# Chunked attention and a squared-ReLU feed-forward on one core: store queues, score slots, and the share of early Strassen differences

## The chip, the cores and the metric

The kernel runs on one core of one Trainium2 chip. Its engines have queues of their own and run side by side: PE (TensorE, matmuls and transposes), DVE (VectorE), ACT (ScalarE), POOL (GpSimd) and SP (SyncE, which here only issues DMAs). The metric is the device time of one execution in microseconds, and the number that counts is the median of the runs.

## The reference

Attention within chunks of 64 tokens comes first; its heads are laid side by side and go through a feed-forward layer with a squared ReLU. There are 8 sequences of 576 tokens, 8 heads of 64, a model width of 512, and 2048 hidden features.

```python
scores = scale * np.matmul(q_c, k_c.transpose(0, 1, 2, 4, 3))   # chunks of 64 x 64
attn = softmax(scores)
x = np.matmul(attn, v_c)            # -> (4608 tokens, 512)
h = np.maximum(x @ w_in, 0.0)       # w_in: 512 x 2048
out = h * h @ w_out                 # w_out: 2048 x 512, float32
```

## The kernel before

**Tiling.** The 4608 tokens form 18 groups of 256 tokens (4 chunks each), and two groups form a block: nine blocks of 512 tokens, 0 to 8. While PE computes the feed-forward layer of block j, the attention of block j+1 is woven in, and the q, k and v of block j+2 are loaded.

**One block.** `ffn_in` (line 392) has 16 units, one for each tile of 128 hidden features: four matmuls of 512 columns accumulate over the model width (line 399), ACT takes the ReLU out of PSUM (line 410), and the square is written to `gT` in bf16, by DVE (line 415) or for three of the tiles by ACT (line 413). The ReLU results have three buffers, the PSUM banks of the units four. From block 2 on, the tiles are taken in the order `FT_EARLY`, in which a few tiles of the lower and the upper half of the hidden features come first.

`ffn_out` (line 436) multiplies by `w_out` with one level of a Strassen scheme: seven products of quarter size, each of 16 matmuls in two steps of eight (line 466). Five of them take a difference of two quarters of `gT` as their left side: d5, d2, d1, d6, d7, in the order in which they are wanted. DVE makes these differences (`difference`, line 384) into tiles called `w_st`. A part of each, the first `N_EARLY` of its eight feature tiles, is made within `ffn_in`, in the queue behind the square of unit 8 (lines 417 to 420). The rest is made at the start of `ffn_out` and between its products (`rest_of`, line 445). The products are, in order, a22 into bank n, a11 into bank m, d5 into n, d2 into m, d1 into n, d6 into m, d7 into n. Between them the banks are read out: n1 and n2 by ACT, the sum w and the output quarters c21, c12 and c22 by DVE (line 431), c11 by ACT (line 546). Each quarter of the output is stored as soon as it is made (`store`, line 482).

**Block 0 and block 1** differ: block 0 uses plain matmuls for the output (`ffn_out_by_ft`), block 1 runs `ffn_in` in two halves of 256 columns and 32 shorter units.

**Attention steps of a group.** In the code: C casts q and k to bf16 (on POOL for groups under 8, else on ACT); TD transposes them with a DMA on SP (line 268; the first groups are transposed by PE instead: TA, TE, TQ, TK); SC computes the scores and ACT takes their exponentials (lines 291 and 302); AV multiplies by the values and DVE divides by the row sums, two steps for each half group, which I call a value division (lines 318, 325, 326); XT transposes the result to `xT`, the input of the next block's `ffn_in` (by PE and a copy for groups under 6, lines 345 and 350; by a DMA on SP from there on, line 339).

**The order of the work** is written out by hand. Each yield of `ffn_in` and `ffn_out` is a slot, and a table gives the slot behind which each attention step is put. Slots 0 to 15 follow the units of `ffn_in`, and 16 to 29 the half products of `ffn_out`. From block 2 on the table is this (the two numbers are those of the two groups); one load is issued on SP at each slot named in `go_slots`:

```python
slots = {SC: (8, 8), AV: (11, 15), XT: (14, 18), C: (18, 20), TD: (20, 23)}
if j == 2:
    slots = {SC: (8, 10), AV: (12, 15), XT: (15, 18), C: (20, 23), TD: (22, 25)}
```

SP issues all loads and the DMA transposes in program order. The stores of the output are issued by POOL; in the last block, where each quarter is stored in two halves of 128 tokens or at once, the two halves of c11 go out on ACT and SP.

Of the kernel before, what the change touches and what calls it, by code (L numbers as in the profile page):

```python
# [17 lines left out]
def kernel(  # L18
# [9 lines left out]
    nc = tc.nc  # L28

    B, H, S, D = q.shape  # L30
# [4 lines left out]
    n_hp = H // 2  # L35
# [296 lines left out]
    def transpose_x(g):  # L332
        j, c = place[g]
        if j not in xTs:
            xTs[j] = att_pool.tile([128, BT // 128, n_dt, 128], BF16, name="xT", bufs=2)
        x = state.pop(("x", g))
        dst = xTs[j][:, c // 128:c // 128 + 2].rearrange("p t h q -> p (t h) q")
        if g >= FIRST_DMA_X:
            nc.sync.dma_start_transpose(out=dst, in_=x.rearrange("p t h a d -> p (t h a d)"))
            return  # L340
        ps = ps_att.tile([128, 1024], FP32, name="ps_att")
        psb = ps.bitcast(BF16)[:, 0:1024].rearrange("p (b q) -> p b q", q=128)
        for t in range(2):
            for hp in range(n_hp):
                nc.tensor.transpose(  # L345
                    out=psb[:, t * n_hp + hp, :],
                    in_=x[:, t, hp].rearrange("p a d -> p (a d)"),
                    identity=ident)
        copy = nc.vector.tensor_copy if g == blocks[1][0] else nc.scalar.copy
        copy(out=dst, in_=psb)  # L350

    C, TD = cast_qk, transpose_qk_dma
    SC, AV, XT = scores, values, transpose_x
# [31 lines left out]
    FT_ORDER = [*range(n_ft // 2, n_ft), *range(n_ft // 2)]  # L385


    N_EARLY = 2
    FT_EARLY = [ft + h for ft in range(N_EARLY) for h in (n_ft // 2, 0)]
    FT_EARLY += [ft for ft in FT_ORDER if ft not in FT_EARLY]  # L390

# [44 lines left out]
    def ffn_out(j):  # L436

        last = j == len(blocks) - 1
        a11, a12, a21, a22 = quarters(j)

        def rest_of(name):
            difference(j, name, slice(N_EARLY if (name, j) in state else 0, HF))
            return state[name, j]

        n_tt = HT // 128
        banks = {}  # L450

        def chain(name):
            tiles = [ps_ffn.tile([128, 512], FP32, name="ps_ffn")
                     for _ in range(n_tt if last else 1)]
            banks[name] = [(tiles[t], 0, HD, t) for t in range(n_tt)] if last else [
                (tiles[0], 0, n_tt * HD, None)]
            return [tiles[t][:, 0:HD] if last else tiles[0][:, t * HD:(t + 1) * HD]
                    for t in range(n_tt)]

        def product(name, a, b, first):  # L460
            if first:
                state["chain", name] = chain(name)
            outs = state["chain", name]
            for t in range(n_tt):
                for i in range(HF):
                    nc.tensor.matmul(  # L466
                        out=outs[t],
                        lhsT=a[:, i, t * 128:(t + 1) * 128],
                        rhs=b[:, i, :],
                        start=(first and i == 0 and (last or t == 0)), stop=(i == HF - 1),  # L470
                        skip_group_check=True)
                yield

        def parts(name):
            for tile_, lo, n, t in banks[name]:
                at_ = (t or 0) * HD
                yield tile_[:, lo:lo + n], slice(at_, at_ + n), t

        def kept(name):
            return ffn_pool.tile([128, n_tt * HD], FP32, name=name)  # L480

        def store(dma, o_sb, half, col, t):
            g = blocks[j][half]
            b, s0 = chunks[g][0]
            t0 = b * S + s0
            if not is_whole(g):

                for p in range(2):
                    dma.dma_start(
                        out=out.rearrange("(b s) d -> s b d", s=S)[  # L490
                            s0:s0 + CH, b + p:b + 4:2, col:col + HD],
                        in_=o_sb[p * CH:(p + 1) * CH].rearrange("p (t d) -> p t d", d=HD))
            elif t is None:
                dma.dma_start(  # L494
                    out=out[t0:t0 + HT, col:col + HD].rearrange("(t p) d -> p t d", p=128),
                    in_=o_sb.rearrange("p (t d) -> p t d", d=HD))
            else:
                dma.dma_start(
                    out=out[t0 + t * 128:t0 + (t + 1) * 128, col:col + HD],
                    in_=o_sb[:, t * HD:(t + 1) * HD])  # L500

        def o_tile():
            return ffn_pool.tile([128, n_tt * HD], FP32, name="o_sb", bufs=4)

        d5 = rest_of("d5")
        d2 = rest_of("d2")
        yield from product("n", a22, b11_p_b21, True)
        n1 = kept("n1")
        for ps, cols, t in parts("n"):
            nc.scalar.copy(out=n1[:, cols], in_=ps)  # L510
        yield from product("m", a11, b12_p_b22, True)
        w = kept("nm")
        for ps, cols, t in parts("m"):
            add(nc.vector, w[:, cols], ps, n1[:, cols])
        d1 = rest_of("d1")
        yield from product("n", d5, b22, False)
        n2 = kept("n2")
        for ps, cols, t in parts("n"):
            nc.scalar.copy(out=n2[:, cols], in_=ps)
        d6 = rest_of("d6")  # L520
        if j == 1:
            d7 = rest_of("d7")
        yield from product("m", d2, b11, False)
        c21 = o_tile()
        for ps, cols, t in parts("m"):
            add(nc.vector, c21[:, cols], w[:, cols], ps, ALU.subtract)
            store(nc.gpsimd, c21, 1, 0, t)
        if j > 1:
            d7 = rest_of("d7")
        yield from product("n", d1, b11_m_b22, False)  # L530
        s = kept("n1")
        for ps, cols, t in parts("n"):
            add(nc.vector, s[:, cols], ps, n2[:, cols], ALU.subtract)
        c12 = o_tile()
        add(nc.vector, c12, w, n2, ALU.subtract)
        store(nc.gpsimd, c12, 0, HD, None)
        yield from product("m", d6, b11_p_b12, False)
        c22 = o_tile()
        for ps, cols, t in parts("m"):
            add(nc.vector, c22[:, cols], ps, s[:, cols])  # L540
            store(nc.gpsimd, c22, 1, HD, t)
        yield from product("n", d7, b21_p_b22, False)
        c11 = o_tile()
        for ps, cols, t in parts("n"):
            copy = nc.vector.tensor_copy if t else nc.scalar.copy
            copy(out=c11[:, cols], in_=ps)  # L546
            store(nc.gpsimd if t is None else nc.sync if t else nc.scalar, c11, 0, 0, t)

    def ffn_out_by_ft(j):

# [76 lines left out]
    for j, grps in enumerate(blocks):  # L627
# [15 lines left out]
        elif j == 1:  # L643
            loads = itertools.chain(*map(v_pieces, nxt), *map(qk_pieces, far))
            go_slots = [*range(22, 27), *range(28, 48)]
            for slot, f in ((1, TK), (4, SC), (7, AV), (12, XT)):
                at(slot, f, grps[1])
            for i, g in enumerate(nxt):
                for slot, f in ((16 + 4 * i, C), (21 + 6 * i, TD), (36 + i, SC), (38 + 2 * i, AV),
                                (41 + 2 * i, XT)):  # L650
                    at(slot, f, g)
            for i, g in enumerate(far):
                at(36 + 4 * i, C, g)
                at(42 + 3 * i, TD, g)
            at(2, sum_quarters(b11_p_b12, b11, b12), None)
            at(12, sum_quarters(b12_p_b22, b12, b22), None)
            at(20, sum_quarters(b21_p_b22, b21, b22), None)
            phases = [ffn_in(1, [(0, 256, FT_ORDER), (256, 256, FT_ORDER)]), ffn_out(1)]
        else:
            loads, go_slots = pieces(far), range(32)  # L660
            slots = {SC: (8, 8), AV: (11, 15), XT: (14, 18), C: (18, 20), TD: (20, 23)}
            if j == 3:
                go_slots = [*range(6), *range(13, 32)]
            if j == 2:
                loads = itertools.chain(*map(v_pieces, nxt), loads)
                slots = {SC: (8, 10), AV: (12, 15), XT: (15, 18), C: (20, 23), TD: (22, 25)}
                go_slots = [*range(16), 23, 24, *range(26, 36)]
            for f in (SC, AV, XT):
                for i, g in enumerate(nxt):
                    at(slots[f][i], f, g)  # L670
            for f in (C, TD):
                for i, g in enumerate(far):
                    at(slots[f][i], f, g)
            phases = [ffn_in(j, [(0, BT, FT_EARLY)]), ffn_out(j)]
        slot = 0
# [41 lines left out]
```

## Time and profile before

| what | us |
|---|---|
| median of 9 runs (lowest, highest) | 284.67 (283.17, 290.31) |
| the profiled execution | 283.25 |
| its span, from the first to the last instruction | 281.1 |
| PE busy | 268.7 |
| DVE busy | 189.4 |
| ACT busy | 161.6 |
| POOL busy | 55.6 |

Times within the profile are in us from the start of the span. Block 2 starts on PE at 82.85, block 3 at 110.84, block 4 at 138.88, block 5 at 166.97, block 6 at 195.00, block 7 at 223.04 and block 8 at 251.07; from block 3 on they are 28.03 to 28.09 apart. A line of the groups gives source line, engine, operation, output and inputs, shapes and count, then the busy time and the mean of one in ns, then the idle time before. A line of waits gives the waiting engine and line, what it waited for, and the total, the number of times and the longest wait. Waits are told by the instruction that waited; a name with a q (SPq, POOLq) is the queue that issues.

### The profile page before, as it was taken

How to read it: one execution, taken by the hardware profiler on the slowest of the kernel's cores; microseconds unless marked ns; L12 is line 12 of the kernel's file. 1: busy time of each engine (PE TensorE's matmuls, PEld its weight loads, DVE VectorE, ACT ScalarE, POOL GpSimd, SP SyncE). 2: the span in 40 equal slices, each digit the busy share in tenths (PEclk: the TensorE clock that was granted, in tenths of full speed). 3: DMA queues.
4: the chain of work that ended last, by engine and by line, in shares of the span. 5: the costliest groups of instructions: out<-in, count | busy, mean ns of one | idle time of the engine just before them, and what ended most of it. 6: DMA issues, size and time to landing. Idle time of an engine off the chain costs nothing.

```text
span 281.1 us, 7197 instructions
## 1 busy us (share of the span) xinstructions
PE 268.7 (96%) x2951; PEld 175.3 (62%) x2954; DVE 189.4 (67%) x338; ACT 161.6 (58%) x277; POOL 55.6 (20%) x92
## 2 busy tenths in 40 slices
PE   1999999999999999999999999999999999999994
PEld 1554444778774487448744874487448744874583
DVE  1254614899953885599559955995599559955982
ACT  1558705786349763976197619761976197119610
POOL 2038834240170003000400040004000400060012
PEclk9999999999999999999999999999999999999999
DMA  7999999999999999989999899669897980341003
GB/s 202 241 327 332 373 352 246 312 227 214 228 224 251 224 219 190 247 188 227 218 281 235 189 244 263 118 140 225 212 248 174 212 163 10 67 113 39 0 38 113
DMA packets 140816, 57.09 MB, mean 203 GB/s; under 512 B 110640, under 2 KB 137520, under 8 KB 140784
## 3 DMA queue, kind: packets, MB, share of 16 engines
q1 hardware_dynamic: 137744, 47.33, 76.6%
q0 software_dynamic: 2896, 9.18, 10.1%
q8 instruction: 23, 0.38, 0.6%
q10 hardware_dynamic: 144, 0.13, 0.1%
q14 instruction: 9, 0.07, 0.1%
HBM read 36.70 MB, written 9.44 MB: 164 GB/s over the span
## 4 chain that ended last, share of the span: by engine, by line
PE 58%; DVE 23%; ACT 7%; issue 4%; SPq 4%; DMA 2%; POOL 0%; ACTq 0%; DVEq 0%
PE ps_ffn L466 27%; PE ps_ffn L399 24%; DVE gT L415 10%; ACT rl L410 6%; DVE x L326 6%; DVE w_st L384 6%; PE ps_ffn L556 5%; DMA w_st<-in_moe_w_in_dram 2%; SPq L106 1%; SPq L148 1%; SPq L152 1%; DVE rec L325 1%; ACT gT L413 1%; PE ps_att L345 1%; PE ps_att L291 1%
## 5 line engine op out<-in xcount | busy, mean ns | idle before, releaser
L399 PE MATMUL ps_ffn<-xT,w_in_bf 128*128 128x512 bf16 (+1 forms) x648 | 129.3, 356 | 0.6 <-POOL w_in_bf L170 0.3
L415 DVE TENSOR_TENSOR gT<-rl 128x512 bf16<-128x512 f32 (+2 forms) x130 | 73.9, 604 | 53.9 <-ACT rl L410 53.8
L410 ACT ACTIVATE rl<-ps_ffn 128x512 f32<-128x512 f32 (+2 forms) x162 | 85.3, 548 | 22.4 <-PE ps_ffn L399 20.6
L399 PEld LDWEIGHTS <-w_in_bf 128*128 128x128 bf16 x648 | 61.8, 98 | 58.1 <-POOL w_in_bf L170 0.5
L466 PEld LDWEIGHTS <-w_st 128*128 128x128 bf16 x640 | 61.8, 98 | 9.0 <-DVE w_st L384 1.8
L384 DVE TENSOR_TENSOR w_st<-gT 128x1536 bf16<-128x1536 bf16 (+2 forms) x75 | 50.3, 721 | 0.0
L466 PE MATMUL ps_ffn<-w_out_bf,w_st 128*128 128x256 bf16 x384 | 45.9, 273 | 0.4
L494 POOL DMA_DIRECT2D out_dram<-o_sb x25 | 17.8, 714 | 127.4 <-DVE o_sb L431 122.8
L466 PE MATMUL ps_ffn<-w_sum,w_st 128*128 128x256 bf16 x256 | 29.6, 273 | 0.0
L546 ACT COPY o_sb<-ps_ffn 128x512 f32<-128x512 f32 (+1 forms) x8 | 4.5, 558 | 40.9 <-PE ps_ffn L466 40.9
L466 PEld LDWEIGHTS <-gT 128*128 128x128 bf16 x256 | 24.5, 98 | 3.3
L326 DVE TENSOR_TENSOR x<-ps_att,rec 128x512 bf16<-128x512 f32 x36 | 24.9, 692 | 1.2
L302 ACT ACTIVATE e<-ps_att 128x1024 bf16<-128x1024 f32 x18 | 17.8, 1023 | 6.0 <-PE ps_att L291 6.0
L413 ACT ACTIVATE gT<-rl 128x512 bf16<-128x512 f32 (+2 forms) x32 | 18.4, 576 | 1.0
L466 PE MATMUL ps_ffn<-w_sum,gT 128*128 128x256 bf16 x128 | 15.3, 273 | 0.0
L466 PE MATMUL ps_ffn<-w_out_bf,gT 128*128 128x256 bf16 x128 | 15.3, 273 | 0.0
L556 PE MATMUL ps_ffn<-w_out_bf,gT 128*128 128x512 bf16 x61 | 14.2, 379 | 0.3 <-issue 0.2
L170 POOL CAST w_in_bf<-w_st 128x512 bf16<-128x512 f32 (+2 forms) x12 | 9.9, 851 | 17.3 <-DMA w_st<-in_moe_w_in_dram 17.3
L510 ACT COPY n<-ps_ffn 128x512 f32<-128x512 f32 (+1 forms) x9 | 4.8, 538 | 12.0 <-PE ps_ffn L466 12.0
L318 PEld LDWEIGHTS <-e 64*64 64x64 bf16 x576 | 6.5, 107 | 7.4 <-ACT rl L410 2.5
L259 ACT CAST qkb<-q_sb 128x1024 bf16<-128x1024 f32 x10 | 10.5, 1048 | 0.0
L262 ACT CAST qkb<-k_sb 128x1024 bf16<-128x1024 f32 x10 | 10.5, 1046 | 0.0
(53 smaller groups left out, 157.1 us busy)
## 6 DMA issues: line engine op xcount, KB each, us to landing
q_sb<-in_q_dram SPq DMA_DIRECT2D x16, 512.0 KB, 6.1
out_dram<-o_sb POOLq DMA_DIRECT2D x29, 256.0 KB, 5.1
k_sb<-in_k_dram SPq DMA_DIRECT2D x24, 256.0 KB, 6.3
ve_sb<-in_v_dram SPq DMA_DIRECT2D x32, 128.0 KB, 4.1
w_st<-in_moe_w_in_dram SPq DMA_DIRECT2D x8, 512.0 KB, 6.3
w_st<-in_moe_w_out_dram SPq DMA_DIRECT2D x8, 512.0 KB, 5.8
vo_sb<-in_v_dram SPq DMA_DIRECT2D x24, 128.0 KB, 3.6
k_sb<-in_k_dram SPq DMA_DIRECT2D x4, 512.0 KB, 6.8
```

What stands on the lines that cost most here:

```text
L259: copy(out=qkb[:, 0].rearrange("p (i h d) -> p i h d", i=2, h=H), in_=q_sb.rearrange("p (h i d) -> p i h d", h=H, i=2))
L262: copy(out=qkb[:, 1], in_=k_sb)
L302: nc.scalar.activation(out=e_out, in_=s_in, func=AF.Exp, scale=scale)
L326: nc.vector.tensor_tensor(out=x[:, t].rearrange("p h a d -> p a h d"), in0=o[:, :, :, 0:D], in1=rec.to_broadcast([128, 2, n_hp, D]), op=AL ...
L384: nc.vector.tensor_tensor(out=state[name, j][:, part], in0=x, in1=y, op=ALU.subtract)
L399: nc.tensor.matmul(out=h[:, 0:n], lhsT=w_in_bf[:, dt, ft * 128:(ft + 1) * 128], rhs=xT[:, c // 128:(c + n) // 128, dt, :], start=(dt == 0) ...
L410: nc.scalar.activation(out=rl[:, 0:n], in_=h[:, 0:n], func=AF.Relu)
L413: nc.scalar.activation(out=gT[:, ft, c:c + n], in_=rl[:, 0:n], func=AF.Square)
L415: nc.vector.tensor_tensor(out=gT[:, ft, c:c + n], in0=rl[:, 0:n], in1=rl[:, 0:n], op=ALU.mult)
L466: nc.tensor.matmul(out=outs[t], lhsT=a[:, i, t * 128:(t + 1) * 128], rhs=b[:, i, :], start=(first and i == 0 and (last or t == 0)), stop=( ...
L494: dma.dma_start(out=out[t0:t0 + HT, col:col + HD].rearrange("(t p) d -> p t d", p=128), in_=o_sb.rearrange("p (t d) -> p t d", d=HD))
L556: nc.tensor.matmul(out=o_ps[tt], lhsT=gT[:, ft, tt * 128:(tt + 1) * 128], rhs=w_out_bf[:, ft, :], start=(ft == 0), stop=(ft == n_ft - 1))
```

## The change

It has five parts.

- **Early share.** `N_EARLY` goes from 2 to 3: three of the eight tiles of each difference are made within `ffn_in`, and five are left for `ffn_out`. The order of the hidden tiles follows from it.
- **Stores.** In blocks 2, 3 and 8 the output stores are issued by SP in place of POOL. In blocks 2 and 3 they stand in SP's program order where the code makes them: behind the q,k transposes, except that the first store of block 2 comes between its two.
- **Last copy.** In block 8, the second half of c11 is copied by DVE and ACT, half of the columns each, and stored by SP and ACT, half each.
- **Slots.** In block 1, the values and XT of group 3 move from slots 7 and 12 to 8 and 13, and XT of groups 4 and 5 from 41 and 43 to 42 and 43. In block 4, scores of group 11 move from slot 8 to 11, the values of group 10 from 11 to 12, and its XT from 14 to 15.
- **xT copy.** The copy of `xT` of group 2 out of PSUM is split between DVE and ACT.

```diff
@@ transpose_x
-        copy = nc.vector.tensor_copy if g == blocks[1][0] else nc.scalar.copy
-        copy(out=dst, in_=psb)
+        if g == blocks[1][0]:
+            nc.vector.tensor_copy(out=dst[:, 0:n_hp], in_=psb[:, 0:n_hp])
+            nc.scalar.copy(out=dst[:, n_hp:], in_=psb[:, n_hp:])
+        else:
+            nc.scalar.copy(out=dst, in_=psb)
@@
-    N_EARLY = 2
+    N_EARLY = 3
@@ ffn_out
+        queue = nc.sync if last or j in (2, 3) else nc.gpsimd
...
-            store(nc.gpsimd, c21, 1, 0, t)
+            store(queue, c21, 1, 0, t)
...
-        store(nc.gpsimd, c12, 0, HD, None)
+        store(queue, c12, 0, HD, None)
...
-            store(nc.gpsimd, c22, 1, HD, t)
+            store(queue, c22, 1, HD, t)
...
         for ps, cols, t in parts("n"):
-            copy = nc.vector.tensor_copy if t else nc.scalar.copy
-            copy(out=c11[:, cols], in_=ps)
-            store(nc.gpsimd if t is None else nc.sync if t else nc.scalar, c11, 0, 0, t)
+            if not t:
+                nc.scalar.copy(out=c11[:, cols], in_=ps)
+                store(nc.scalar if last else queue, c11, 0, 0, t)
+                continue
+            b, s0 = chunks[blocks[j][0]][0]
+            for copy, dma, c in ((nc.vector.tensor_copy, nc.sync, 0),
+                                 (nc.scalar.copy, nc.scalar, HD // 2)):
+                half = c11[:, cols][:, c:c + HD // 2]
+                copy(out=half, in_=ps[:, c:c + HD // 2])
+                dma.dma_start(
+                    out=out[b * S + s0 + t * 128:b * S + s0 + (t + 1) * 128, c:c + HD // 2],
+                    in_=half)
@@ the slots of block 1
-            for slot, f in ((1, TK), (4, SC), (7, AV), (12, XT)):
+            for slot, f in ((1, TK), (4, SC), (8, AV), (13, XT)):
...
-                                (41 + 2 * i, XT)):
+                                (42 + i, XT)):
@@ the slots from block 2 on
+            elif j == 4:
+                slots.update({SC: (8, 11), AV: (12, 15), XT: (15, 18)})
```

## The prediction

> **What bounds the kernel now.** I began with the page, part 1 and the slices of part 2 (one digit is the busy tenth of a 7 us slice).
>
> ```profile
> PE 268.7 (96%) x2951; PEld 175.3 (62%) x2954; DVE 189.4 (67%) x338; ACT 161.6 (58%) x277; POOL 55.6 (20%) x92
> ...
> PE   1999999999999999999999999999999999999994
> ...
> DMA  7999999999999999989999899669897980341003
> ```
>
> PE is busy from the second slice to the last, and matmuls of 256 columns start every 109 ns: outside the ends only its waits and interruptions can be won. DMA is nearly full too up to slice 32, so transposes and stores share a scarce thing. Then the waits of the whole span (total us, times, longest):
>
> ```profile
> DVE gT L415 <- ACT rl L410: 53.8, 49, 3.0
> ...
> PEld L466 <- DVE w_st L384: 1.8, 5, 0.4
> ```
>
> PE waits five times for a difference, and no more than 0.4 us at a time. The chain that ended last, cut to 173–187 us (block 5; start, us, work), shows what stands before one such wait:
>
> ```profile
> 174.21 0.59 ACT rl L410
> ...
> 174.82 1.29 DVE gT L415 x2
> 176.12 1.68 DVE w_st L384 x5
> 177.79 0.98 DVE gT L415 x2
> ...
> 185.39 0.88 DVE w_st L384
> 186.27 0.05 issue
> 186.32 0.72 PE ps_ffn L466 x5
> ```
>
> From 174.82 to 186.27 DVE has no pause: 11.34 of the 11.5 us between 174.8 and 186.3 are busy. It runs two squares, the five early differences, seven squares, four value divisions and the rest of d5; then PE goes on. The same chain ends at 130.19, 158.28, 186.32, 214.35 and 242.39, blocks 3 to 7. So here DVE, 67% busy over the span, sets the time. PE's gap, counted between matmul starts, is 0.24–0.25 us in each. Block 2 (squares of bf16, 0.42 us) has d5 ready 0.3 us early, and block 8, with no attention, has no such gap.
>
> Prices of differences, from the groups by form (busy, mean ns):
>
> ```profile
> L384 DVE TENSOR_TENSOR w_st<-gT 128x1536 bf16<-128x1536 bf16 x35 | 32.1, 951 | 0.0
> ...
> L384 DVE TENSOR_TENSOR w_st<-gT 128x512 bf16<-128x512 bf16 x35 | 12.3, 419 | 0.0
> ```
>
> Back to back they start 0.335 us (512) and 0.87 us (1536) apart, so 0.52 ns an element.
>
> The end, first from the timeline after 275.5, then from the answer for the last source line:
>
> ```profile
> 277.15 0.42 DVE L546 COPY o_sb<-ps_ffn 128x256 f32<-128x256 f32 x1 [1.32 <-PE ps_ffn L466]
> 277.61 0.39 SPq L498 DMA_DIRECT2D out_dram<-o_sb  x1
> ```
> ```profile
> L712 POOLq DRAIN  x3: 45/102/4177, 276.1 to 280.8; - x3
> ```
>
> The last store lands at 279.34, and SP is through at 279.49. But POOL, having issued five of the last block's stores, drains for 4.18 us, from 276.10 to 280.28; everything after follows that.
>
> **What the Trainium skill says.** "DVE: scalar operands, raw-bit mode, write accounting and state across instructions", section 5 (Flops that outlive an instruction), calls DVE's queue one in-order queue. The trace agrees: d5's rest starts only at 185.31, behind the divisions. "VectorE: DVE Perf Modes", The perf-mode tier table, gives a bf16 sum of two tensors of 2048 elements 1224 ns; here it is 1219. "DMA: Bandwidth & Descriptors", Issuing engines are not separate DMA queues: the issuer changes only who spends the issue time, the transfers share the same 16 engines. It fits: the q,k transpose issued at 108.36, with three stores in flight, needed 10.1 us from issue to landing, against 5.4 at 188.43. "SBUF — State Buffer", Who interferes with whom: two SBUF inputs on DVE collide with GpSimd reads, not with its writes. A difference at 190.41 beside a POOL store issue took 0.95 as elsewhere, so moving stores off POOL gives DVE nothing.
>
> **Three eighths early.** Take block 5. The order of hidden tiles becomes 8, 0, 9, 1, 10, 2, 11, 12, …, so ACT squares units 2, 4, 7 instead of 2, 4, 6.
> - ACT: relu of unit 7 can start at 173.96 (PE ends the unit at 173.90); its square follows at 174.58, and relu of unit 8, before at 174.78, at 175.12 (square to relu 0.54). Ends 175.70.
> - DVE: square of unit 6 at 173.71, in idle time; square of unit 8 at 175.74; the differences start at 176.34, not 176.03: +0.31.
> - Five of 768 elements, by the slope 0.468 us each, take 2.34 instead of 1.69: +0.65. The next square starts at 178.68, not 177.72. Its relu, delayed to 177.41–178.02, is there.
> - The rest is as long as before, so d5's rest starts 0.96 later, at 186.27. With 1280 elements it takes 0.82 (before 0.95) and ends at 187.09; 0.07 later (as before) PE goes on, at 187.16.
> - PE wants it one matmul later, after three early tiles, at 185.86 + 3 × 0.109 = 186.19. It waits 0.97 instead of 0.245: **+0.73 us**.
>
> The saved 0.13 on d2, d1, d6 and d7 buys nothing, as nobody waits for them. What follows still fits: the sum w is done at 188.43, and product m·d2 wants it at 188.58. The three relu buffers delay only relu 15, with PE not waiting. Block 2 has 1.2 us of DVE idle time after its early differences, so 0. Block 8 wants d5 only at 268.35 and has it by 267.9, so 0. Five blocks: 5 × 0.73 = **+3.6**. Both ends for the 768-element price, which no row shows: one start each 0.335 us, as with 512, would leave +0.1 a block; 0.55 each without overlap, +1.15. The slope between two rows is the better guess.
>
> **Block 1.** PE waits 0.23 for exp of group 3 at 54.75; AV one slot later puts a 0.44 us unit before it, and the wait goes: −0.23. Within XT of group 3 PE waits 0.6 for the second division; both move by about 0.2, so it stays. XT of group 4 waits 0.16 at 77.92 for a PSUM bank released at 78.23; a slot later (0.9 us) it is free: −0.16. The xT copy of group 2 is one DVE copy of 0.69 ending at 50.14. Halves take 0.42 on DVE and 0.58 on ACT, but ACT is in an output copy until 49.59, so its half ends near 50.15: 0. Together **−0.4**, bounds 0 and −0.8.
>
> **End.** All POOL stores of block 8 go to SP (five issues of 0.4–0.6, spread over 271–276, before nothing but the last store), so POOL's drain is early. Halving the last copy makes 0.29 on DVE, 0.27 on ACT (by their slopes), and two landings: SP 277.48 + 1.74 = 279.2, ACT 277.46 + 2.13 (its landing before) = 279.6. End after 279.6 instead of 280.28: **−0.7**, bounds −0.3 and −1.0.
>
> **Stores of blocks 2 and 3.** Eight issues of 0.7 leave POOL, where nothing waits for them, and enter SP at about 0.6 each: 2.4 us a block. Behind them stand v loads, then the next block's loads and XT. Only the first store of block 2 stands ahead of a q,k transpose (slot 24 before 25). The bytes are the same on engines already full, so loads behind arrive about when they did. The transposes ahead land sooner, and margins are thin: by the semaphore increments qkT of group 9 landed at 118.48 (scores at 118.7), xT of 9 at 138.73 (block 4 starts at 138.88), qkT of 11 at 146.25 (scores about 146.8). Scores of group 11 at slot 11 add three units, 2.6 us, to the last. In this execution PE never waited there, so 0, bounds −0.5 and +2. In block 4, values at 12 and 15 leave DVE the same chain, so +0.73 holds.
>
> **Sum.** The profiled execution took 283.25 us (span 281.1, 2.15 around): 283.25 + 3.6 − 0.4 − 0.7 = 285.75. The median of the nine is 1.42 above it. Transposes with margins of 0.15–0.5 us can be late in such runs, and the change loosens them; the start, DMA-fed, can be late also and is not touched. I leave half: 285.75 + 0.7 ≈ **286.4**.
>
> **Rivals.**
> 1. *The early differences run in DVE's idle time.* They need only units 0 to 5, and DVE idles between 174.40 and 175.74. Taken up at 174.40 they would end at 176.74; only relu 9, now ending at 178.02, would hold the chain, by 0.3 us, and the wait would grow by 0.33 − 0.13 − 0.11 = 0.09 a block. The time would be 284.67 + 5 × 0.09 − 1.1, and less the half excess: 283.4. It decides as soon as the growth stays under 0.36 us a block (five of it then pay less than the 1.1 and 0.7 won). Against it: line 417 queues them behind the square of unit 8, and the queue is in order.
> 2. *Late transposes were the median's whole excess.* Then all of 1.42 goes: 285.8, within 0.5%. For: the margins above. Against: the first matmuls of weights, at 18.56, wait for DMA as well.
> 3. *SP becomes late.* XT of block 3 and the loads for block 6 stand behind stores that wait for DVE and ACT. If xT of group 9 lands 1–2 us later, block 4 starts late: 287.3 to 288.5. For: SP reached that XT at 134.18, its input ready since 129.3. Against: equal bytes, and block 3's stores then come behind it.
>
> **How the numbers follow.** Measurement tells 0.5%, 1.42 us, from no change: slower is over 286.09, faster under 283.25. The forecast's chance is 0.57 (285.7 to 287.3; slower 0.42, same 0.15); rival 1, 0.20 (282.6 to 284.2; faster 0.10, same 0.10); rival 2, 0.12 (same); rival 3, 0.11 (slower). Sums: faster 0.10, same 0.37, slower 0.53. The range 283.0 to 287.9 leaves out about 0.07 below and 0.07 above; the forecast's own is 285.7 to 287.3.
>
> **What would show it.** Right: PE's waits for w_st about 1 us each in blocks 3 to 7, some 4.8 us in all, differences of 768 elements near 550 ns, block starts near 28.75 us apart (28.03 before), POOL's last drain short, XT's wait at 77.9 gone. Wrong: w_st waits still at 0.25, or new PE waits on xT or qkT transposes.

## The result, and the profile after

The median went from 284.68 us (52 runs, 282.6 to 291.15) to **286.66 us** (17 runs, 286.13 to 288.86), a ratio of **1.0095 [1.0073, 1.0118]**. The kernel became slower, by nearly 1%. The ratio counts only executions within 1.5% of the fastest of their kernel (40 of the 52 of the kernel before, with a median of 284.1); the two medians above alone would give 1.007. The profiled execution took 286.70 us, with a span of 284.9; it lies at the median, while that of before, 283.25, lies 1.4 us under its own. Line numbers moved with the edit: the differences are now at line 388, the square at 419, `ffn_out`'s matmul at 472.

The page after, part 1:

```profile
PE 270.7 (95%) x2951; PEld 176.4 (62%) x2954; DVE 187.6 (66%) x338; ACT 162.6 (57%) x279; POOL 48.0 (17%) x79
```

The averages say next to nothing: DVE is even a little less busy than before (187.6 against 189.4). The time is in the waits of the whole span:

```profile
DVE gT L419 <- ACT rl L414: 56.2, 47, 3.1
...
PEld L472 <- DVE w_st L388: 3.6, 5, 0.8
```

DVE waits 2.4 us longer for ReLUs (53.8 before), which costs nothing by itself, as long as nobody then waits for DVE. PE still waits five times for a difference, now 3.6 us in all instead of 1.8. The chain that ended last, cut to block 5 (start, us, work), shows what stands before one such wait:

```profile
176.87 0.57 ACT rl L414
...
177.47 0.69 DVE gT L419
178.16 2.34 DVE w_st L388 x5
180.50 1.81 DVE gT L419 x3
...
188.08 0.74 DVE w_st L388
188.82 0.05 issue
188.87 1.16 PE ps_ffn L472 x9
```

Five differences take 2.34 us where they took 1.68, and the last piece of d5 ends 0.05 us before PE goes on. Measured from the block's first matmul (168.53 us; 166.81 in the kernel before, where the 166.97 given above is the end of block 4's work), the five start 9.63 us in (9.31 before), d5's rest 19.55 (18.58 before), and PE goes on at 20.34 (19.51 before). Blocks 3 to 7 now take 28.76 or 28.77 us each; before it was 28.03 to 28.09.

The groups by form (busy, mean ns) give the two new sizes:

```profile
L388 DVE TENSOR_TENSOR w_st<-gT 128x1280 bf16<-128x1280 bf16 x35 | 27.5, 819 | 0.0
...
L388 DVE TENSOR_TENSOR w_st<-gT 128x768 bf16<-128x768 bf16 x35 | 17.0, 552 | 0.0
```

Block 1 begins later than before. The timeline around its start (start, us, engine, work, then the idle time before and what ended it):

```profile
50.17 0.42 DVE L351 COPY xT<-ps_att 128x512 bf16<-128x512 bf16 x1 [0.63 <-PE ps_att L345]
...
50.63 0.59 ACT L352 COPY xT<-ps_att 128x512 bf16<-128x512 bf16 x1 [0.32 <-DVE xT L351]
...
51.26 0.38 PE L403 MATMUL ps_ffn<-xT,w_in_bf 128*128 128x256 bf16 x2 [0.56 <-ACT xT L352]
```

The two halves of the copy run one after the other: ACT, idle, waits for DVE's half, and PE for ACT's. PE's pause here grew from 0.406 to 0.753 us. The same thing happens at the end, in the timeline after 281 us:

```profile
281.06 0.29 DVE L560 COPY o_sb<-ps_ffn 128x128 f32<-128x128 f32 x1 [1.32 <-PE ps_ffn L472]
281.38 0.33 SPq L561 DMA_DIRECT2D out_dram<-o_sb  x1
281.38 0.27 ACT L560 COPY o_sb<-ps_ffn 128x128 f32<-128x128 f32 x1 [0.82 <-DVE o_sb L560]
281.72 0.34 ACTq L561 DMA_DIRECT2D out_dram<-o_sb  x1
```

The stores landed at 283.71 and 283.89, 2.33 and 2.16 us after those starts. POOL's long drain is no longer the end; the answer for the last source line has it at 256.3, under block 8:

```profile
L730 POOLq DRAIN  x3: 45/93/3918, 256.3 to 284.6; - x3
```

The two spans differ by 3.85 us (284.92 against 281.07), and the distances between block starts say where:

| stretch | us, after less before |
|---|---|
| up to block 0's start | +0.25 |
| block 0, to block 1's start | +0.81 (0.35 the xT copy, 0.40 a wait for a load of k) |
| block 1 | −0.74 (0.39 the slots, 0.35 a cast, see e9) |
| block 2 | about 0 |
| blocks 3 to 7 | +3.59 |
| block 8 and the tail | −0.06 |

### The profile page after: what moved, and what is told of

Same layout as the page of the kernel before. It is cut to its first block, busy times and chain, and to the rows that moved or that the text cites. A ratio compares the mean times of both kernels' runs of the same rounds, so it can differ in the third digit from the quotient of the medians.

```text
span 284.9 us, 7206 instructions
## 1 busy us (share of the span) xinstructions
PE 270.7 (95%) x2951; PEld 176.4 (62%) x2954; DVE 187.6 (66%) x338; ACT 162.6 (57%) x279; POOL 48.0 (17%) x79
## 3 DMA queue, kind: packets, MB, share of 16 engines
q1 hardware_dynamic: 140768, 50.15, 78.3%
## 4 chain that ended last, share of the span: by engine, by line
PE 63%; DVE 17%; DMA 9%; SPq 6%; issue 2%; ACT 1%; POOL 1%
PE ps_ffn L472 29%; PE ps_ffn L403 28%; DVE gT L419 7%; DMA k_sb<-in_k_dram 5%; DMA w_st<-in_moe_w_in_dram 4%; DVE x L326 4%; DVE w_st L388 4%; PE ps_ffn L572 2%; SPq L106 2%; SPq L152 1%; SPq L148 1%; PE ps_att L291 1%; PE ps_att L318 1%; POOL w_in_bf L170 1%; DVE rec L325 1%
## 5 line engine op out<-in xcount | busy, mean ns | idle before, releaser
L419 DVE TENSOR_TENSOR gT<-rl 128x512 bf16<-128x512 f32 (+2 forms) x130 | 73.1, 601 | 56.2 <-ACT rl L414 56.2
L388 DVE TENSOR_TENSOR w_st<-gT 128x1280 bf16<-128x1280 bf16 (+2 forms) x75 | 50.3, 721 | 0.0
L500 POOL DMA_DIRECT2D out_dram<-o_sb x16 | 11.5, 717 | 133.0 <-DVE o_sb L435 130.3
L472 PEld LDWEIGHTS <-gT 128*128 128x128 bf16 x256 | 24.5, 98 | 3.3
L572 PEld LDWEIGHTS <-gT 128*128 128x128 bf16 x64 | 6.0, 98 | 7.0
```

What stands on the lines that cost most here:

```text
L388: nc.vector.tensor_tensor(out=state[name, j][:, part], in0=x, in1=y, op=ALU.subtract)
L419: nc.vector.tensor_tensor(out=gT[:, ft, c:c + n], in0=rl[:, 0:n], in1=rl[:, 0:n], op=ALU.mult)
L472: nc.tensor.matmul(out=outs[t], lhsT=a[:, i, t * 128:(t + 1) * 128], rhs=b[:, i, :], start=(first and i == 0 and (last or t == 0)), stop=( ...
L500: dma.dma_start(out=out[t0:t0 + HT, col:col + HD].rearrange("(t p) d -> p t d", p=128), in_=o_sb.rearrange("p (t d) -> p t d", d=HD))
L572: nc.tensor.matmul(out=o_ps[tt], lhsT=gT[:, ft, tt * 128:(tt + 1) * 128], rhs=w_out_bf[:, ft, :], start=(ft == 0), stop=(ft == n_ft - 1))
```

## The experiments

My theory was that the early share alone costs about 3.6 us, by DVE's chain, and that the rest of the change gains. Against it stood that later stores or scores cost something too, and, for the differences, that their size matters less than what they stand behind. Medians are given with lowest and highest and the number of runs; ratios are to the kernel before.

### What the early share costs

**e1: the changed kernel with two tiles early again.**

```diff
-    N_EARLY = 3
+    N_EARLY = 2
```

> The changed kernel with 2 of 8 tiles early, as before; all else changed. Theory (the vector engine's chain to d5 sets five blocks): PE's gaps at d5 go back from 0.97 to 0.25 us, blocks 3 to 7 are 28.03 us apart, and the time falls by 5 x 0.73 = 3.65, to about 283.0, 0.6% under the kernel before. Rival (SyncE becomes late with the stores in its queue, hidden in the changed kernel by the slower PE): new PE waits on xT, qkT or loads, 284 to 286, with a wide spread. Rival (the early share is not the cause): 286.7 as changed.

Measured: 282.98 us (282.01 to 288.2, 22 runs), ratio 0.9953 [0.9929, 0.9976]. Waits of the whole span:

```profile
PEld L472 <- DVE w_st L388: 1.7, 5, 0.4
```

The wait for differences is what it was before the change. The share costs 286.66 − 282.98 = 3.7 us in the median, and the remaining four parts together make the kernel faster.

**e2: the kernel before, with the early share alone.**

```diff
-    N_EARLY = 2
+    N_EARLY = 3
```

> The kernel before with 3 of 8 tiles early and nothing else. Theory: gaps at d5 of 0.97 us in blocks 3 to 7, blocks 28.76 apart, lowest run 282.6 + 3.65 = 286.2; the median is 288.3 if the spread of before stays as it is, and 286.5 to 287 if a slower PE gives late transposes time and the spread shrinks. Rival (the early share costs nothing by itself): 284.7.

Measured: 288.96 us (287.03 to 293.52, 6 runs), ratio 1.0133 [1.0081, 1.0186]. The profiled execution, at 292.46, was the second longest of the six. Waits of the whole span:

```profile
PEld L291 <- DMA qkT<-qkb: 3.9, 4, 1.5
...
PEld L399 <- DMA xT<-x: 3.2, 1, 3.2
PEld L466 <- DVE w_st L384: 3.1, 4, 0.8
```

PE's gap at d5 is 0.73 us here as well in blocks 3, 5 and 7, so the price of the share doesn't depend on the other parts. New beside it are PE's waits for DMA transposes: scores (line 291) wait for `qkT`, and `ffn_in` (line 399) once 3.2 us for `xT`. I had thought that a slower PE might itself give late transposes time to land, so that the spread would shrink. It didn't: the six lie between 287.03 and 293.52 (the changed kernel's 17 between 286.13 and 288.86), so something else in the change must have removed these waits.

**e4: the changed kernel, its early differences put behind the square of unit 6.** They then stand in DVE's idle time, not behind the square of unit 8.

```diff
-            if fts is FT_EARLY and u == 8:
+            if fts is FT_EARLY and u == 6:
```

> The changed kernel, its early differences queued behind the square of unit 6 instead of unit 8, where the vector engine is idle. Theory: they run from 174.4 on in terms of block 5 of the kernel before, only relu 9 then holds the chain; the gap at d5 falls from 0.97 to 0.34 us, and the time by 5 x 0.64 = 3.2, to about 283.5. Rival (the wait is bound by the amount of work on the vector engine, not by its place): 286.7 as changed.

Measured: 284.1 us (283.03 to 287.5, 20 runs), ratio 0.9979 [0.9952, 1.0006]; the profiled execution took 283.5. Waits of the whole span:

```profile
PEld L472 <- DVE w_st L388: 1.8, 4, 0.5
```

PE's gap at d5 falls from 0.73 to 0.33 us in blocks 3, 5, 6 and 7 (block 4, with its later slots, has none), a gap of 0.2 us that PE has before it in the changed kernel, at the values of the second group, goes, and blocks come 28.13 to 28.19 us apart. So most of the cost isn't the additional work on DVE but its place in the queue: three tiles early cost 2.6 us less behind unit 6 than behind unit 8 (286.66 − 284.1). They are then still no better than two tiles behind unit 8 (e1).

**e8: the changed kernel, ACT squaring units 2, 4 and 6 again in place of 2, 4 and 7.**

```diff
-    SQUARES_ON_ACT_EARLY = (9, 10, 12)
+    SQUARES_ON_ACT_EARLY = (9, 10, 11)
```

> The changed kernel with the third ACT square at unit 6 (tile 11) instead of unit 7 (tile 12). Theory (0.31 of the 0.73 comes from that square standing before relu 8): the gap at d5 is 0.97 - 0.31 = 0.66 us, 0.41 above that of the kernel before, and blocks 3 to 7 are 28.45 apart; time of one execution about 285.1. Rival (the square's place does not matter): 0.97, 28.76 apart, 286.7.

Measured: 284.21 us, one execution; PE's gap at d5 is 0.63 to 0.645 us in blocks 3, 5, 6 and 7. Waits of the whole span:

```profile
PEld L472 <- DVE w_st L388: 3.2, 5, 0.8
```

The wait at d5 has hardly moved, but the gap of 0.2 us at the values of the second group is gone here too, and the blocks come 28.43 us apart in place of 28.76. So the 0.31 us by which the later square of ACT delays the differences comes back in full. What is left over 28.03 is the larger size. The single time is no measure of this: five blocks are worth 1.6 us of the 2.5, and a shorter tail most of the rest.

### What the stores and the slots give

**e5: e1 with the stores of blocks 2 and 3 back on POOL.**

```diff
-        queue = nc.sync if last or j in (2, 3) else nc.gpsimd
+        queue = nc.sync if last else nc.gpsimd
```

> The run with 2 of 8 early, with the stores of blocks 2 and 3 on GpSimd again; block 4's later scores and the last block's SyncE stores stay. Theory A (the stores running beside the transposes make them late, and the changed queue cures it): lowest run as with 2 of 8 early, 282.0, but a wider spread and a median near 284 to 284.5, with PE waits on xT or qkT. Theory B (the later scores of group 11 cure it): median stays at 283.0. Rival (the queue of the stores makes no difference): 283.0 too.

Measured: 284.27 us (282.32 to 288.15, 14 runs), ratio 0.9992 [0.9955, 1.0029]. Lowest times are close (282.32 and 282.01 in e1), medians 1.3 us apart (1.1 by the ratios). Waits of the whole span:

```profile
PEld L403 <- DMA xT<-x: 4.1, 2, 2.9
```

The profiled execution (286.49) lost its time at the starts of blocks 5 and 7, where `ffn_in` waited 1.0 and 2.82 us for `xT`. Its chain from 215 to 229 us:

```profile
215.83 5.95 PE ps_ffn L472 x53
221.78 5.36 DMA xT<-x
...
227.18 1.90 PE ps_ffn L403 x8
```

A DMA transpose stands in the chain where PE should pass from one block to the next. Most of its lateness is in its issue: SP, which has loads ahead of it, came to the two transposes of `x` 24.07 and 25.45 us into block 6, against 21.31 and 22.68 in e1's profiled execution, and they then took 5.0 and 5.4 us to land, against 3.3.

The traces point to the stores' queue as what changes how long a transpose is in flight. `qkT` of group 9, transposed beside the stores of block 2, landed 10.1 us after its issue in the kernel before, 7.8 in e5 and 4.6 in e2, all with stores on POOL; in the ten traces with these stores on SP it took 3.8 to 4.7 us (4.4 in the changed kernel, 110.82 to 115.18). The 4.6 shows that stores on POOL don't always slow it. The late waits of e5 are two to four blocks behind the stores that were moved. That full DMA engines carry a backlog so far, and so make SP late, is my inference; the traces show only where it came out. The intervals of e5 and e1 overlap a little, so that the stores are worth 1.1 to 1.3 us is likely rather than certain.

**e6: e1 with block 4's slots as before (scores of group 11 at 8).**

```diff
-            elif j == 4:
-                slots.update({SC: (8, 11), AV: (12, 15), XT: (15, 18)})
```

> The run with 2 of 8 early, with block 4's slots as in the kernel before (scores of group 11 at slot 8). Theory A (the stores' queue is the cure): median stays near 283.0. Theory B (the later slot is the cure): a wider spread, median 284 to 284.5, the wait in some executions at the scores of group 11 in block 4. If both are needed, both of these runs are slow.

Measured: 282.81 us (281.88 to 286.26, 22 runs), ratio 0.9967 [0.9941, 0.9993]. Nothing is lost without the later slots: the transposes land in time by then, and the margin that the slots add isn't used. It isn't free either. Block 4 takes 28.03 us here and 28.39 in e1 (28.38 in e3, which has the later slots too): PE leaves `ffn_in` once more for the scores of group 11 and waits 0.16 us at the values. The changed kernel doesn't show this, since its block 4 takes 28.76 us like its neighbours; there DVE's chain sets the block either way. So the early share costs 3.7 us in blocks 3 to 7 measured against e6, and 3.3 against e1.

**e9: the kernel before, with only the stores of blocks 2, 3 and 8 on SP and block 1's slots.**

```diff
+        queue = nc.sync if last or j in (2, 3) else nc.gpsimd
...
-            store(nc.gpsimd, c21, 1, 0, t)
+            store(queue, c21, 1, 0, t)
...
-            for slot, f in ((1, TK), (4, SC), (7, AV), (12, XT)):
+            for slot, f in ((1, TK), (4, SC), (8, AV), (13, XT)):
...
-                                (41 + 2 * i, XT)):
+                                (42 + i, XT)):
```

> The kernel before with only two parts of the change: the stores of blocks 2, 3 and 8 on SyncE, and block 1's slots. Theory: no more PE waits on transposes than with 2 of 8 early, block 1 shorter by 0.75 us with no split xT copy, the end 0.65 us shorter: lowest 281.6, median 282.5, 0.8% under the kernel before. Rival (the split copies or block 4's slots were needed): 283 or more.

Measured: 282.72 us (281.58 to 289.31, 21 runs), ratio 0.9968 [0.9941, 0.9995]. As far as the medians tell, these two parts hold all the gain that the other four had in e1 (282.98). The tail, from the last matmul's start to the end, is 3.58 us against 4.22 before. Block 1, however, took 32.51 us, as before (32.48), where the changed kernel has 31.74. DVE's timeline in block 1 of e9, and then POOL's:

```profile
55.28 1.88 DVE L415 TENSOR_TENSOR gT<-rl 128x256 bf16<-128x256 bf16 x4 [0.56 <-ACT rl L410]
```
```profile
55.83 1.18 POOL L259 CAST qkb<-q_sb 128x1024 bf16<-128x1024 f32 x1 [5.57 <-DMA q_sb<-in_q_dram]
```

Four squares take 1.88 us, beside a cast on POOL. In e3 (below), the same four, with the cast over by 55.64, take 1.11:

```profile
55.30 1.11 DVE L415 TENSOR_TENSOR gT<-rl 128x256 bf16<-128x256 bf16 x4 [0.56 <-ACT rl L410]
```

In the kernel before, a square at 55.71 took 1.06 us instead of 0.28, beside a cast from 55.58 to 56.63; in the changed kernel the cast came at 57.82, past the squares. The rest of the cast sets what a square loses. That square ended 0.14 us after its cast; so did e9's at 56.10 (1.06 us), and so did the first of e3's four, begun at 55.30 with 0.34 us of the cast to go, which took 0.48. Over all thirteen traces, 44 of the 48 squares of 256 columns that began beside such a cast ended 0.14 us after it, while the 29 value divisions that began beside one, with one input in PSUM, took 0.69 us as always. This fits the Trainium skill, "SBUF — State Buffer", Who interferes with whom: a DVE instruction with two SBUF inputs collides with a GpSimd instruction that reads SBUF. When the cast starts depends on when its load lands.

So block 1's −0.74 in the profiled pair is in part luck of the loads. The trace of e2 tells the parts apart: it has block 1's slots as before, but its first cast comes at 57.29, after the squares, and block 1 took 32.13 us. The waits for the exponentials of group 3 and within XT of group 4, which the prediction wanted to remove, are still there and are gone in the changed kernel. That gives 0.35 us to the cast and 0.39 to the slots, from one execution each. With the cast on the squares, as in e9, the slots gained nothing.

### What the halved copies give

**e3: e1 with the xT copy of group 2 and the last copy whole again.**

```diff
-            nc.vector.tensor_copy(out=dst[:, 0:n_hp], in_=psb[:, 0:n_hp])
-            nc.scalar.copy(out=dst[:, n_hp:], in_=psb[:, n_hp:])
+        copy = nc.vector.tensor_copy if g == blocks[1][0] else nc.scalar.copy
+        copy(out=dst, in_=psb)
...
+            copy = nc.vector.tensor_copy if t else nc.scalar.copy
+            copy(out=c11[:, cols], in_=ps)
+            store(queue if t is None else nc.sync if t else nc.scalar, c11, 0, 0, t)
```

> As the run with 2 of 8 early, and with the xT copy of group 2 and the last copy whole on the vector engine again, the last store on SyncE. Theory (the two halves of a copy out of one PSUM bank run one after the other, as the trace of the changed kernel shows, so that splitting costs): block 1 starts 0.35 us earlier, and the last store lands near 1.74 us after its issue instead of 2.3, so the end comes 0.6 earlier: 0.9 to 1.0 under the run with 2 of 8 early, about 282.1. Rival (the halves gain what they should): 0.2 over it.

Measured: 283.07 us (281.67 to 286.88, 22 runs), ratio 0.9969 [0.9944, 0.9994]. PE's pause before block 1 is back at 0.405 us, and the lowest time is 0.34 us under e1's, as the pause says. The median isn't better, where I had expected 282.1: a third of a microsecond doesn't show in it. The tail is 3.57 us with the whole copy and 3.56 (e1) with the halves: halving the last copy gains nothing. In the changed kernel and e4, two of the six profiled executions with halves, the last two stores took 2.16 to 2.6 us to land instead of under 1.6.

### Versions that might beat both

**e7: two tiles early, but behind unit 6, whole copies, and later scores and values in every block from 3.** The idea was to put e4's place of the differences and e3's copies on top of e1.

```diff
-            if fts is FT_EARLY and u == 8:
+            if fts is FT_EARLY and u == 6:
...
-            slots = {SC: (8, 8), AV: (11, 15), XT: (14, 18), C: (18, 20), TD: (20, 23)}
+            slots = {SC: (8, 11), AV: (12, 15), XT: (15, 18), C: (18, 20), TD: (20, 23)}
```

`N_EARLY` is 2, as in e1, and the copies are as in e3.

> 2 of 8 early, differences behind unit 6, both copies whole, stores as in the changed kernel, and block 4's slots (scores 8 and 11, values 12 and 15, transposes 15 and 18) in all blocks from 3 on. Theory (the exp of the second group no longer stands before relu 9, and the differences run in the vector engine's idle time, so the chain to d5 is 0.4 us shorter): the gaps of 0.24 at d5 go, 5 x 0.24 = 1.2 us under the run with whole copies: 281.9, lowest 280.5. Rival (transposes at slot 15 and values at 12 are late in some block, or values wait for PSUM banks): no gain, 283.

Measured: 284.18 us (283.2 to 285.82, 14 runs), ratio 1.0014 [0.9983, 1.0045]: a miss of 2.3 us. PE's gap at d5 did fall, to 0.18 us. But a gap of 0.16 at the values is new, and scores of two groups in two places instead of one cost PE one more turn out of `ffn_in` and back, 93 and 95 ns. Blocks come 28.38 us apart, 0.35 more than before. Block 4 of e1, with the same slots and the differences behind unit 8, took 28.39 us, with a gap of 0.19 at d5. So the slots account for the whole loss, and for the smaller gap; beside them, the place of the differences gave nothing. Two tiles behind unit 6 with the slots as before were not run.

**e10: e9 with the third of ACT's squares given to unit 13 in place of unit 6.** This takes a square from DVE between the early differences and d5's rest.

```diff
-    SQUARES_ON_ACT_EARLY = (9, 10, 12)
+    SQUARES_ON_ACT_EARLY = (9, 10, 5)
```

> As the stores-and-block-1 run, with the third ACT square at tile 5 (unit 13, where ACT idles) instead of tile 12 (unit 6). Theory (the vector engine's unbroken chain to d5 is what PE waits for, so 0.6 us of it handed to ACT late ends the wait): the gaps of 0.24 us at d5 in blocks 3 to 7 vanish, 28.03 apart becomes 27.8, 5 x 0.24 = 1.2 us less: median 281.3. Rival (relus 14 and 15, behind that square on ACT, become late and take it back): 282.5.

Measured: 282.69 us (281.31 to 290.3, 17 runs), ratio 0.9953 [0.9923, 0.9982]. The chain of block 5 in the profiled execution (281.32):

```profile
175.15 2.70 PE ps_ffn L399 x12
177.85 0.39 PE ps_att L318 x32
178.24 3.56 PE ps_ffn L399 x16
181.80 0.39 PE ps_att L318 x30
182.20 6.87 PE ps_ffn L468 x62
```

DVE is gone from it: PE follows on PE, no wait of PE for `w_st` is left, and blocks are 27.78 to 27.80 us apart (block 5: 27.95) instead of 28.03. In the median, though, nothing is left of the 1.2 us that five such blocks should give (282.72 in e9). The lowest time gained 0.27 us (281.31 against 281.58). No long execution of this kernel was profiled, so what takes the rest back is not shown; late transposes are the suspect that the next run tries.

**e11: e10 with the stores of blocks 4 to 7 on SP too.**

```diff
-        queue = nc.sync if last or j in (2, 3) else nc.gpsimd
+        queue = nc.sync if j > 1 else nc.gpsimd
```

> As the late-square run, with the stores of blocks 4 to 7 on SyncE too. Theory (stores beside transposes make those late in some executions): a narrower spread, median nearer to the lowest, 281 or less. Rival (SyncE's queue is then late with loads and transposes): PE waits on xT or qkT, 282 to 284.

Measured: **282.04 us** (280.98 to 285.65, 22 runs), ratio 0.9935 [0.9908, 0.9962], the fastest of all and below both kernels, but not the 281 expected. Transposes did land sooner: the last, `qkT` of group 17, took 4.1 us, against 9.2 in e10. Yet in the profiled execution (284.46) block 6 took 30.59 us, 2.80 more than blocks 3, 5 and 7. Its chain from 210 to 227 us:

```profile
210.40 6.05 DMA k_sb<-in_k_dram
...
216.53 1.04 ACT qkb L262
217.58 0.49 ACT n L521
...
218.11 1.92 PE ps_ffn L468 x16
...
220.51 4.18 DMA xT<-x
```

A load of k came late, its cast on ACT waited for it, the copy of n2 stood behind the cast, and PE waited 1.4 us for that copy. Then PE waited 1.4 us for `xT`. SP had issued the two transposes of `x` 24.99 and 26.36 us into the block, where e10 issued them at 21.45 and 22.82; in flight they took 3.3 and 4.2 us. Ahead of them SP had four stores of block 5, between 1.8 and 8.4 us into block 6, among the loads. This is the rival of this run: SP's queue was late with loads and transposes. One execution doesn't tell how often that happens, nor whether the stores alone did it, as blocks 4 and 5 hold four stores each on SP in this trace and took 27.98 and 27.79 us. The interval of this ratio overlaps that of e10; that e11 is the better of the two is not proven.

## Why the prediction was right, and where it wasn't

286.4 us was forecast and 286.66 measured. Split by the runs, the median moved by +3.7 (e1 to the changed kernel) and by about −1.7 (the remaining parts); forecast were +3.6 and −1.8. The second number was right by luck: two errors cancel.

- **Three eighths early: right, step by step.** Forecast were +0.31 for the start of the differences, +0.96 for d5's rest, +0.84 for PE's going on, and +0.73 a block. Measured from the block's start they are +0.32, +0.97, +0.83 and +0.73. Blocks 3 to 7 sum to +3.59 and block 2 to about 0. The price of a 768-element difference, taken from the slope between two rows, was 0.468 us from start to start; five took 2.34. e8 undid the first term alone and got 0.33 a block back.
- **Where the wait would show: wrong in part.** About 1 us at d5 and some 4.8 in all was forecast; PE waits 0.73 there and 3.6 in all. The prediction took PE to arrive at d5 as early as before. The late chain delays the value divisions too, so PE already loses about 0.2 us at the values of the second group (in blocks 3, 5, 6 and 7), waiting for a PSUM bank that DVE has still to read, and reaches d5 that much later. In block 4, with its later slots, it waits 0.40 us at the values and 0.13 at d5. The sum is the same, since DVE sets it. The forecast followed PE only at the end of the chain.
- **Rival 1 (differences in idle time): its arithmetic held, its condition did not.** It put the growth at 0.09 us a block for differences taken up in the idle time; e4 moved them there and found a gap of 0.33 against 0.245. In the changed kernel they stand behind the square of unit 8, in order, as the prediction read from the code.
- **Block 1: the failed step is "its half ends near 50.15: 0".** It let the halves of the xT copy run side by side. They ran in series, and cost 0.35 us. This could have been known: the Trainium skill, "PSUM — Partial Sum Buffer", PSUM bank collisions raise a hardware error, says that no two engines may access one bank on the same partitions at once, two reads included, and that the compiler puts a dependency between them. `xT`'s source is 1024 bf16 elements, one bank of the 2 KiB that the same page gives. The trace agrees (ACT idle 0.32 us, released by DVE's half), and e3 took the 0.35 back. The −0.4 of the slots was right (0.39, from e2). A wait of 0.6 us within XT of group 3, which was to stay, went as well: it came from the cast beside the squares, and e2, with the old slots and a later cast, lacks it too.
- **End: −0.7 forecast, −0.06 in the profiled pair.** That POOL's drain leaves the end is right, and e1, e3 and e9 have tails 0.64 to 0.66 us shorter than before. In the changed kernel's own profiled execution the last store took 2.16 us to land where e1's took under 1.6, which used up the gain. The halves again ran in series and gave nothing.
- **Stores of blocks 2 and 3: the mechanism was right, the size too small.** The transposes did land sooner (group 9's in 4.4 us against 10.1). "In this execution PE never waited there, so 0" was true of that execution and not of the median: e5 puts the stores at 1.1 to 1.3 us of it. The Trainium skill's sentence on issuers ("DMA: Bandwidth & Descriptors", Issuing engines are not separate DMA queues), on which the step leaned, says that the transfers share the same engines whoever issues them. These runs don't contradict it, but it isn't all: which queue a store stands in decides here whether it is in flight beside a transpose or behind it.
- **"I leave half" of the excess: wrong, and it carried the sum.** The median's excess over the lowest time went from 2.1 us (1.5 with the median of 284.1) to 0.5 (286.66 − 286.13), most of it or nearly all, as rival 2 had it; 0.7 had been forecast. Against that, the lowest times rose by 3.5 us (282.6 to 286.13), where 3.6 − 0.4 − 0.7 = 2.5 had been forecast for an undisturbed execution: the end gained nothing in the profiled pair, and the xT copy cost 0.35. So some 0.8 us too little was asked of the excess and some 1.0 too much of block 1 and the end, and in the median these nearly cancel. Rival 2 would have named the mechanism and still missed the time, as it kept the 1.1 of block 1 and the end.
- **Rival 3 (SP becomes late)** is out for the change: in the traces of the changed kernel and of e1 PE waits for a DMA transpose no longer than 0.2 us, and e5, which unloads SP, is slower, not faster. With the stores of all blocks from 2 on in SP's queue (e11), its mechanism does appear.

What stays open: what makes SP late in e5's long execution, and why e10's 1.2 us don't reach the median.

## What to carry to other kernels

- Work split off "to be early" costs more by its place in an in-order queue than by its length: three tiles cost 3.7 us behind one square and 2.6 us less two units sooner, so find the idle time first and put the work in it.
- Where a median lies above the lowest time, price a change twice, once in the undisturbed execution and once for what makes executions long; here one part moved only the first (the share), another mainly the second (the stores).
- Before splitting a copy over two engines, ask whether both halves lie in one PSUM bank.
- A margin can cost: later slots for scores and values took 0.35 us of each block that they were put in, unless something slower hid it.

## What the runs showed of the hardware

- Halves of one bank on DVE and ACT ran in series, 0.42 and 0.59 us, where one whole copy on DVE took 0.69.
- A last store of 128 rows and 128 columns landed 1.56 to 1.59 us after its issue in e1, e6 and e8, and after 2.16 to 2.6 in the changed kernel and e4, for the same data; stores of 128 rows and 256 columns took 1.71 in e3, e7, e9 and e10. A tail can't be read from one execution to better than half a microsecond.
- A square on DVE that began beside a POOL cast ended 0.14 us after the cast, so that it took up to 1.13 us instead of 0.28 (0.48 with 0.34 us of the cast to go). Value divisions, which have an input in PSUM, took 0.69 us beside a cast as without one.
- With the output stores on the queue that issues the transposes, one q,k transpose took 3.8 to 4.7 us from issue to landing in ten traces; with them on POOL's queue it took 10.1, 7.8 and 4.6 in three, with the same bytes to move.
